# Transposes of a tail's normalized tiles enter TensorE's order 1600 planned nanoseconds later

## The chip, the cores and the metric

The kernel runs on one core of a Trainium2 chip. The metric is the device time of one execution in microseconds (us). One core has five engines with an instruction queue each: TensorE (PE in the profile; its weight loads are listed as PEld), VectorE (DVE), ScalarE (ACT), GpSimd (POOL) and SyncE (SP), which issues most DMA transfers. Every queue is worked off in the order in which the program wrote it; an instruction whose inputs are not there yet holds up all that stands behind it in its queue.

## The reference

The program is one block with adaptive layer norm: an attention followed by a mixer. S = 2048 rows, D = 512 columns, H = 32 heads of 16, F = 1792, all in float32.

```
mod = silu(c) @ w_mod                       # six rows: sa, ca, ga, sb, cb, gb
h = layernorm(x) * (1 + ca) + sa
x = x + ga * attention(h, wqkv, wo)         # softmax over 2048 keys, 32 heads
h = layernorm(x) * (1 + cb) + sb
# mixer B(h):
g  = gelu(layernorm(h) @ w1)                # then four column groups shifted by +1, -1, +2, -2 rows
x1 = h + shifted(g) @ w2
x  = x + gb * (x1 + gelu(layernorm(x1) @ w3) @ w4)
```

## The kernel before

**Tiling.** Rows are worked in four chunks of 512 (ci = 0 to 3), each of four tiles of 128 rows. The attention runs chunk by chunk over units of two heads. What follows the attention in a chunk is called its tail, a generator `tail(ci)` with a second part `rest(ci)`. Float32 products are made of three matmuls on a high and a low part (lines 359, 361 and 363), so every activation that TensorE reads as an operand is first split into two parts: a copy on ACT (line 353) and a subtraction on DVE (line 349).

**The steps of a tail.** The attention's output `osb` is transposed (tile `xT`) and split into `A`. Then, for each of the chunk's four tiles, `wo` (12 matmuls of 512 columns), the residual, two layer norms on DVE and POOL (`tst`, `tmv`, `trs`) and last an ACT operation that writes the normalized tile `xn` (line 1367). Two tiles are a group. The group's eight transposes (`xT` from `xn`, line 1247, in the helper `transposed`) and their split give the operand `A` of w1 for this group; w1 has 48 matmuls of 256 columns per group, each bank of 12 followed by a gelu chain on ACT, DVE and POOL (lines 1438 to 1460). With both groups through w1, w2 (12 matmuls of 512 columns per tile) follows, another layer norm, and another set of normalized tiles ("xn4") in groups of two or three tiles. Their transposes give the operand of w3. `rest(ci)` alternates w3 and w4 over pieces of F and writes the output. In `rest(0)` the weights of w3 and w4 are also split for the first time ("fresh", lines 1210 to 1212) and stored; all later uses load the split ones.

**Who transposes.** Each group's transposes are a generator of their own, `norm_T(ts, key, i)`. There are 15 of them: two "xn" groups in every tail, one "xn4" group in tail 0 and two in each of the others. The xn4 groups of tails 1 to 3 also wait until the tail before has issued all of w3. The tiles `xn` have few buffers (three for each kind, two for one), and a tile's wo is not started while they are taken; `norm_T` gives its buffers free after its transposes are split.

**What sets the order.** No order is left to a compiler. The program plans its own time with a class `Sched`: `T["P"]` is TensorE's planned time, advanced by a cost for each matmul (`nsq`: 0.4405 ns per column and 6) and by 110 ns for a transpose; `T["A"]`, `T["D"]`, `T["G"]` stand for ACT, DVE and POOL. Work for TensorE comes from a list of generators. `one()` walks the list from its head and advances the first generator that can run by one matmul. A generator that yields a function is held until the function says true; one that yields a number has used that much planned time. `spawn` puts `norm_T` at the head of the list, so it goes ahead of everything else once it is free to run. Behind it stand the tails in order, then the `rest` parts. Work for the other engines is a chain of operations with costs, which are written into their engines' queues as planned time passes; `mark` sets a flag (such as ("xn", t): tile t is normalized) when the chain's planned time is reached. All this happens while the program is written. On the chip there is only the resulting order in each queue, and semaphores.

While the attention runs, tail 0 is fed into TensorE's order in portions: `fill(due)` is called behind some blocks of attention work, with a budget of planned time (in the last stretch 1000 ns a block, spent once 1300 have come together). When the attention is over, its PSUM banks are given back, a new PSUM pool is opened, the tails 1 to 3 are put on the list, and `step()` moves planned time on in steps of 100 ns; if no generator can run in a step, planned time passes and nothing is written.

Of the kernel before, what the change touches and what calls it, by code (L numbers as in the profile page):

```python
# [72 lines left out]
W0G = 1  # L73
WSPL = 1
ZPRIO = 2
NPRIO = 1
HOLD = 0
NLOW = 1
# [243 lines left out]
def cD(n=CH):  # L322
    return n / 0.96 + 69
# [7 lines left out]
def kernel(ctx, tc, A_x, A_wqkv, A_wo, B_w1, B_w2, B_w3, B_w4, c, w_mod, out):  # L331
# [89 lines left out]
    sch = Sched()  # L421
# [806 lines left out]
    def transposed(src, ks, nt, A):  # L1228

        n = nt * P  # L1230
        ks = list(ks)
        if n <= 2 * P:
            ks = [ks[i:i + 2] for i in range(0, len(ks), 2)]
        else:
            ks = [[k] for k in ks]
        left = [len(ks)]

        def one():
            left[0] -= 1
        for kk in ks:  # L1240
            yield sch.room
            b = dbank("xT")
            m = len(kk)
            b3 = b[:, :m * n].rearrange("p (k n) -> p k n", k=m)
            for j, k in enumerate(kk):
                for i in range(nt):
                    te.transpose(b3[:, j, i * P:(i + 1) * P], src(k, i), ident)  # L1247
                    yield 110
            k = slice(kk[0], kk[0] + m)
            sch.chain(*split_ops(A[:, k, 0, :n], A[:, k, 1, :n], b3, 1.0, m * n), (None, 0, one), bank=b)  # L1250
        yield lambda: left[0] == 0

    def spawn(gen, key):

        def run():
            yield from gen
            done.add(key)
        sch.add(run(), 0)
# [24 lines left out]
    def tail(ci):  # L1283
# [25 lines left out]
        def tA(nm, i, n):  # L1309

            t = big["A4" if nm == "A4" and not (end and i) or early else "A"]
            o = (2 * P * i if t is big["A4"] or nm == "A" else 0) * 2 * KT
            return t[:, o:o + 2 * KT * n].rearrange("p (k i n) -> p k i n", k=KT, i=2)
# [61 lines left out]
        def normed(key, t, rs):  # L1375
            tag = xtag(key, t)
            xlive[tag] = xlive.get(tag, 0) + 1
            x = xn[key, t] = (tp if tag == "x4" else fa).tile([P, D], F32, name="xn", tag=tag, bufs=XN[tag])
            y = xbt[t]
            return ln_apply(x, y, rs), mark((key, t))  # L1380

        def xtag(key, t):
            if key == "xn":
                return "xn" if early else "xf"
            return "x4" if ci and t in sub[0] else "xn"
# [4 lines left out]
        def norm_T(ts, key, i):  # L1390

            yield lambda: all((key, t) in done for t in ts) and (key == "xn" or not ci or ("w3", ci - 1) in done)
            An[key, i] = A = tA("A4" if key == "xn4" else "A", i, len(ts) * P)
            yield from transposed(lambda k, j: xn[key, ts[j]][:, k * P:(k + 1) * P], range(KT), len(ts), A)
            xlive[xtag(key, ts[0])] -= len(ts)

        for i, t in enumerate(new):
            yield lambda: ci != 1 or i < HOLD or ("xn4", 2) in done
            yield lambda: sch.room() and xn_room("xn", t) and t in x1t and sch.now() >= arr.get(("x1", t), 0.0) and (ci < 2 or ("z", t - 2 * TPC) in done)
            yield from wo_mm(i, range(KT))  # L1400
            b = banks.pop(i)
            x1 = x1t[t]
            xb = xbt[t] = pool_of(ci).tile([P, D], F32, name="xb", tag="xb", bufs=XBF if pool_of(ci) is fa else XBT)

            def x1_add(x1=x1, b=b):
                dve.tensor_tensor(x1, x1, b, op=OP.add)
                sch.free(b)

            r, m, ops = ln_ops(x1, True)
            r2, ops2 = ln_ops(xb)  # L1410

            def center(xb=xb, x1=x1, m=m, ops=ops):
                ops[0][2]()
                sch.late = sch.put("G", 464, sch.T["D"] - cD() + XX, ops[1][2]) + XX
                dve.scalar_tensor_tensor(xb, x1, m[:, 0:1], cbrow, op0=OP.subtract, op1=OP.mult)

            def scale(xb=xb, r=r):
                dve.scalar_tensor_tensor(xb, xb, r[:, 0:1], sbrow, op0=OP.mult, op1=OP.add)

            go = partial(sch.chain, ("D", cD(), x1_add), ("D", 2 * cD() + 150, center), ("D", cD(), scale), *ops2,  # L1420
                         *normed("xn", t, r2), bank=b)
            go()
            if i % 2:
                spawn(norm_T(grp[i // 2], "xn", i // 2), ("T", ci, i // 2))
# [77 lines left out]
        for si, ts in enumerate(sub):  # L1502
            yield lambda: all(("g", ci, i, n) in done for i in range(1 + (t0 + 1 in ts)) for n in range(4))
            for t in ts:
                yield lambda: sch.room() and xn_room("xn4", t)
                b = dbank("w2")
                yield from rows_mm(b, lambda k, p: g[:, k, p, 130 + (t - t0) * P - SH[k]:][:, :P], w, range(KT), KT)
                xb, x1 = xbt[t], x1t[t]

                def xb_add(xb=xb, b=b):  # L1510
                    dve.tensor_tensor(xb, xb, b, op=OP.add)
                    sch.free(b)

                r, ops = ln_ops(xb)
                z = (("D", cD(), lambda xb=xb: dve.scalar_tensor_tensor(xb, xb, 2.0, gbrow, op0=OP.mult, op1=OP.mult)),
                     ("G", cG(), lambda xb=xb, x1=x1: pool.tensor_tensor(x1, x1, xb, op=OP.add)), mark(("z", t)))
                sch.chain(("D", cD(), xb_add), *ops, *normed("xn4", t, r),
                          (None, 0, lambda z=z: sch.chain(*z, prio=ZPRIO)), bank=b, prio=NPRIO)
            spawn(norm_T(ts, "xn4", si), ("T4", ci, si))
# [211 lines left out]
```

## Time and profile before

| | |
|---|---|
| median of 3 runs | 2020.98 us (2018.84 to 2023.25) |
| profiled execution | 2021.44 us |
| its span, first to last instruction | 2019.7 us |
| mean granted TensorE clock | 0.992 |
| TensorE busy | 1934.4 us (96%) |
| DVE, POOL, ACT busy | 1656.3, 1571.9, 1510.2 us |
| instructions | 41655 |

All rows of the prediction come from the profiled execution. In the timeline a row has the start in us from the span's beginning, the duration, the engine, the line of the kernel, the operation, what it writes and from what, and a count where equal neighbours are merged; brackets hold the idle time of the engine just ahead and what ended it. Matmuls are pipelined, so the cost of one in a row of many is the distance from start to start, which is shorter than its duration. The tails 1 to 3 begin at about 1540 us, behind the attention.

### The profile page before, as it was taken

How to read it: one execution, taken by the hardware profiler on the slowest of the kernel's cores; microseconds unless marked ns; L12 is line 12 of the kernel's file. 1: busy time of each engine (PE TensorE's matmuls, PEld its weight loads, DVE VectorE, ACT ScalarE, POOL GpSimd, SP SyncE). 2: the span in 40 equal slices, each digit the busy share in tenths (PEclk: the TensorE clock that was granted, in tenths of full speed). 3: DMA queues.
4: the chain of work that ended last, by engine and by line, in shares of the span. 5: the costliest groups of instructions: out<-in, count | busy, mean ns of one | idle time of the engine just before them, and what ended most of it. 6: DMA issues, size and time to landing. Idle time of an engine off the chain costs nothing.

```text
span 2019.7 us, 41655 instructions
## 1 busy us (share of the span) xinstructions
PE 1934.4 (96%) x14456; PEld 1162.1 (58%) x14456; DVE 1656.3 (82%) x2979; ACT 1510.2 (75%) x3085; POOL 1571.9 (78%) x1488
## 2 busy tenths in 40 slices
PE   7999999999999999999999999999998999999999
PEld 5755545454444444444444444444455878898998
DVE  6398888879999999999999999999975886556443
ACT  6438987768999999999999999999985544344443
POOL 6349988879999999999999999999996554435222
PEclk9989999999999999999999999999999999999999
DMA  8777675445343434444443435354414676553541
GB/s 295 233 204 192 151 187 155 135 130 124 86 92 87 91 88 83 96 82 97 81 98 75 104 72 107 72 136 126 99 46 158 230 261 265 226 200 116 201 153 68
DMA packets 185508, 278.01 MB, mean 138 GB/s; under 512 B 117104, under 2 KB 127856, under 8 KB 169008
## 3 DMA queue, kind: packets, MB, share of 16 engines
q1 hardware_dynamic: 181792, 267.20, 49.1%
q10 hardware_dynamic: 2304, 4.20, 0.6%
q0 software_dynamic: 1200, 3.93, 0.5%
q8 instruction: 115, 1.88, 0.4%
q14 instruction: 97, 0.79, 0.1%
HBM read 211.81 MB, written 62.91 MB: 136 GB/s over the span
## 4 chain that ended last, share of the span: by engine, by line
PE 61%; DVE 16%; ACT 9%; issue 6%; POOL 4%; DMA 3%; SPq 0%; ACTq 0%; POOLq 0%; DVEq 0%
PE mb L996 13%; DVE mx L992 12%; PE pv L1086 9%; PE sc L1012 8%; ACT pt L1008 7%; PE w L363 5%; PE w L359 5%; PE w L361 5%; PE pv L1083 4%; PE ot L1113 3%; POOL pt L1061 2%; PE xT L1247 1%; POOL trs L1356 1%; PE v L359 1%; DMA wr<-Ws 1%
## 5 line engine op out<-in xcount | busy, mean ns | idle before, releaser
L1061 POOL TENSOR_SCALAR pt<-pt 128x1024 f16<-128x1024 uint16 x953 | 1248.3, 1367 | 79.9 <-ACT pt L1008 76.7
L992 DVE TENSOR_REDUCE mx<-mb 128x1 f32<-128x512 f32 x2048 | 1250.0, 681 | 72.7 <-PE mb L996 63.5
L1008 ACT ACTIVATE pt<-sc 128x512 int32<-128x512 f32 x2048 | 1060.9, 614 | 123.5 <-PE mb L996 97.1
L996 PE MATMUL mb<-kst,qtl 62*128 62x512 f32 x2048 | 781.1, 461 | 20.5 <-ACT pt L1008 10.0
L1012 PE MATMUL sc<-qtl,kst 64*128 64x512 f32 x2048 | 739.3, 449 | 4.6 <-DVE mx L992 1.8
L996 PEld LDWEIGHTS mb<-kst,qtl 62*128 62x128 f32 x2048 | 358.9, 193 | 233.7 <-ACT pt L1008 160.4
L1012 PEld LDWEIGHTS sc<-qtl,kst 64*128 64x128 f32 x2048 | 336.6, 185 | 185.4 <-DVE mx L992 118.7
L1086 PE MATMUL pv<-pt,vst 128*32 128x512 f16 x4096 | 384.8, 397 | 20.6 <-ACT ac L1103 20.6
L1460 POOL TENSOR_TENSOR g<-sq,g 128x256 fp32r<-128x256 f32 (+1 forms) x124 | 96.8, 785 | 188.9 <-ACT g L1459 176.6
L1083 PE MATMUL pv<-pt,vst 128*32 128x512 f16 (+1 forms) x2048 | 220.8, 389 | 2.5 <-POOL pt L1061 2.4
L1086 PEld LDWEIGHTS <-vst 128*32 128x32 bf16 x4096 | 91.8, 93 | 227.2 <-issue 208.8
L361 PE MATMUL w<-A,wr 128*128 128x256 f32 (+1 forms) x520 | 153.4, 295 | 0.3 <-DVE A L349 0.3
L359 PE MATMUL w<-A,wr 128*128 128x256 f32 (+1 forms) x520 | 153.2, 295 | 0.3 <-ACT A L353 0.3
L363 PE MATMUL w<-A,wr 128*128 128x256 f32 (+1 forms) x520 | 153.1, 294 | 0.0
L1456 ACT ACTIVATE sq<-w 128x256 f32<-128x256 f32 (+1 forms) x130 | 52.1, 401 | 127.0 <-PE w L363 117.5
L363 PE MATMUL w<-wr,g 128*128 128x512 f32 x270 | 106.5, 394 | 3.1 <-POOL g L1460 3.1
L359 PE MATMUL w<-wr,g 128*128 128x512 f32 x270 | 106.9, 396 | 1.8 <-DMA wr<-Ws 1.8
L361 PE MATMUL w<-wr,g 128*128 128x512 f32 x270 | 106.1, 393 | 0.0
L1438 DVE SCALAR_TENSOR_TENSOR sq<-sq,w 128x256 f32<-128x256 f32 (+1 forms) x130 | 58.1, 449 | 56.5 <-ACT sq L1458 56.3
L359 PEld LDWEIGHTS w<-A,wr 128*128 128x128 f32 x520 | 98.7, 190 | 1.7 <-ACT A L353 0.5
L361 PEld LDWEIGHTS w<-A,wr 128*128 128x128 f32 x520 | 98.7, 190 | 1.6 <-DVE A L349 0.5
L363 PEld LDWEIGHTS w<-A,wr 128*128 128x128 f32 x520 | 98.6, 190 | 0.5 <-issue 0.5
(156 smaller groups left out, 2131.6 us busy)
## 6 DMA issues: line engine op xcount, KB each, us to landing
wr<-Ws SPq DMA_DIRECT2D x66, 1024.0 KB, 5.2
vst<-Vs SPq DMA_DIRECT2D x64, 768.0 KB, 5.7
kst<-Ks SPq DMA_DIRECT2D x126, 384.0 KB, 6.1
Ws<-wr SPq DMA_DIRECT2D x14, 1024.0 KB, 5.0
qtl<-Qs SPq DMA_DIRECT2D x128, 96.0 KB, 4.3
Vs<-vt SPq DMA_DIRECT2D x32, 384.0 KB, 4.2
Ks<-qk SPq DMA_DIRECT2D x16, 512.0 KB, 3.8
Qs<-qk SPq DMA_DIRECT2D x16, 512.0 KB, 3.0
```

The source lines that it names most:

```text
L359: te.matmul(o, lh, rh, start=first, stop=False)
L361: te.matmul(o, lh, rl, start=False, stop=False)
L363: te.matmul(o, ll, rh, start=False, stop=last)
L992: end = sch.crit("D", 605, e + PX, lambda: dve.reduce_max(mxs[u][:, j, g, c:c + 1], b, axis=AX.X))
L996: return ready, lambda: te.matmul(b, lhs, kst[u % 3][r, c * CH:(c + 1) * CH], start=True, stop=True), after
L1008: ea = sch.crit("A", 480, e + PX, lambda: act.activation(pt[s][:, j], b, AF.Exp))
L1012: return ready, lambda: te.matmul(b, kst[u % 3][r, kt * P:(kt + 1) * P], qst[u][r], start=True, stop=True), after
L1061: e_low[s] = XP["G"] + sch.crit("G", 1345, ready, lambda: pool.tensor_scalar(o, i, 0.5, 1.0, op0=OP.mult, op1=OP.mult))
L1083: te.matmul(acc[r:r + n, :], v[:, kt + i, c:c + n].bitcast(F16), pt[s + i].bitcast(F16)[:, j, 0::2], start=False, stop=kt == NKT - 2, skip ...
L1086: te.matmul(acc[r:r + 32, :], v[:, kt, r:r + 32], pt[s].bitcast(F16)[:, j, 1::2], start=kt == 0, stop=False, skip_group_check=True)
L1113: te.matmul(b[:, t * n:(t + 1) * n], ac[:, t * P:(t + 1) * P], smat.rearrange("p j d -> p (j d)"), start=True, stop=True)
L1460: ("G", cG(n), lambda: pool.tensor_tensor(lo, sq, hi, op=OP.subtract)), (None, 0, end), bank=b)
```

## The change

A constant `TW = 1600.0` is added, and one line in `norm_T`. Once all tiles of the group are marked as normalized, the generator is held until TensorE's planned time has advanced by another 1600 ns; only then does it take its buffer and emit transposes. `sch.wait(t)` returns the function that compares planned time with the time of the call plus t. Nothing else is edited, and every group in every tail is treated alike.

```diff
 ZPRIO = 2
+TW = 1600.0
 NPRIO = 1
...
         def norm_T(ts, key, i):

             yield lambda: all((key, t) in done for t in ts) and (key == "xn" or not ci or ("w3", ci - 1) in done)
+            yield sch.wait(TW)
             An[key, i] = A = tA("A4" if key == "xn4" else "A", i, len(ts) * P)
             yield from transposed(lambda k, j: xn[key, ts[j]][:, k * P:(k + 1) * P], range(KT), len(ts), A)
             xlive[xtag(key, ts[0])] -= len(ts)
```

## The prediction

> **What bounds the kernel now.** I read the page first, then the list of who waited for whom, then TensorE's timeline around each wait, since the change only moves TensorE work.
>
> ```profile
> span 2019.7 us, 41655 instructions
> PE 1934.4 (96%) x14456; PEld 1162.1 (58%) x14456; DVE 1656.3 (82%) x2979; ACT 1510.2 (75%) x3085; POOL 1571.9 (78%) x1488
> ```
>
> TensorE bounds the kernel: it is busy 96% of the span, so a change of order can only win what is left of idle time, or open more. The list of waits says who causes the idle time (total us, times, longest us).
>
> ```profile
> PE xT L1247 <- ACT xn L1367: 14.1, 9, 2.9
> ...
> PE w L363 <- POOL g L1460: 3.1, 2, 2.2
> ...
> PE w L359 <- DMA wr<-Ws: 1.8, 3, 0.9
> ```
>
> In the tails the transposes (xT, line 1247) that wait for the last normalized tile (xn, line 1367) hold most of it: 14.1 us in 9 waits. These are the instructions that the change moves. The timeline shows the nine waits, one of another kind ahead of them, and one group that waits for nothing (start, duration, what; in brackets the idle time before it).
>
> ```profile
> 1539.93 1.09 PE L1247 MATMUL xT<-ident,xn 128*128 128x128 f32 x8 [2.25 <-DVE sq L1438]
> ...
> 1558.70 0.33 PE L1247 MATMUL xT<-ident,xn 128*128 128x128 f32 x1 [0.56 <-ACT xn L1367]
> 1560.60 0.33 PE L1247 MATMUL xT<-ident,xn 128*128 128x128 f32 x1 [1.57 <-ACT xn L1367]
> 1563.87 2.40 PE L1247 MATMUL xT<-ident,xn 128*128 128x128 f32 x10 [2.94 <-ACT xn L1367]
> ...
> 1582.53 0.98 PE L1247 MATMUL xT<-ident,xn 128*128 128x128 f32 x7 [1.54 <-ACT xn L1367]
> ...
> 1605.38 0.98 PE L1247 MATMUL xT<-ident,xn 128*128 128x128 f32 x7 [2.52 <-ACT xn L1367]
> ...
> 1659.21 0.98 PE L1247 MATMUL xT<-ident,xn 128*128 128x128 f32 x7 [1.40 <-ACT xn L1367]
> ...
> 1707.28 0.98 PE L1247 MATMUL xT<-ident,xn 128*128 128x128 f32 x7 [2.04 <-ACT xn L1367]
> ...
> 1790.40 1.91 PE L1247 MATMUL xT<-ident,xn 128*128 128x128 f32 x16
> ...
> 1818.00 0.98 PE L1247 MATMUL xT<-ident,xn 128*128 128x128 f32 x7 [0.59 <-ACT xn L1367]
> ...
> 1832.26 0.98 PE L1247 MATMUL xT<-ident,xn 128*128 128x128 f32 x7 [0.98 <-ACT xn L1367]
> ```
>
> Read with the code, 1558.70 to 1563.87 is tail 0's three-tile second group; 1582.53 and 1605.38 are tail 1's first two groups, 1659.21 and 1707.28 tail 2's, 1818.00 and 1832.26 tail 3's. Each waits because the planner counts the chain from a matmul to its normalized tile shorter than it runs.
>
> **The change part by part.** It adds no instruction and no wait on the chip. The planner's wait only lets other generators emit for 1600 planned ns first. Where none can, TensorE's order stays as it is and the cost is nothing, since planned idle time emits nothing. Where one can, that many matmuls go ahead of the transposes. How many follows from the steps between starts.
>
> ```profile
> 1580.36 0.33 PE L361 MATMUL w<-A,wr 128*128 128x384 f32 x1
> 1580.53 0.34 PE L363 MATMUL w<-A,wr 128*128 128x384 f32 x1
> ...
> 1608.20 0.28 PE L359 MATMUL w<-A,wr 128*128 128x256 f32 x1
> 1608.32 0.28 PE L361 MATMUL w<-A,wr 128*128 128x256 f32 x1
> ```
>
> A step is 0.17 us at 384 columns and 0.12 us at 256, so 1.6 us is 10 or 14 matmuls. With a step of 0.23 us at 512 columns (below) it is 7.
>
> *Tail 0's groups before 1545.* The group at 1539.93 waits 2.25 us for DVE, where the PSUM pool is closed; w1's second half needs these transposes and nothing else is open, so I take 0. The first group stands in the attention; it is the slower rival below.
>
> *Tail 0's three-tile group (1558.70).* When its last tile is normalized, wo of tail 1 opens in the same planned moment and now goes first.
>
> ```profile
> 1557.76 0.39 PE L363 MATMUL w<-wr,g 128*128 128x512 f32 x1
> ...
> 1565.92 0.78 PE L359 MATMUL wo<-wr,A 128*128 128x512 f32 x1
> 1566.49 0.63 PE L361 MATMUL wo<-wr,A 128*128 128x512 f32 x1
> 1566.92 0.63 PE L363 MATMUL wo<-wr,A 128*128 128x512 f32 x1
> ...
> 1569.89 0.40 PE L359 MATMUL wo<-wr,A 128*128 128x512 f32 x1
> 1570.12 0.40 PE L361 MATMUL wo<-wr,A 128*128 128x512 f32 x1
> ...
> 1606.12 0.36 PE L361 MATMUL w<-A,wr 128*128 128x256 f32 x1
> ...
> 1562.50:1563.00 0.50, 0.00 (x0) 1.00 0.00 0
> 1563.00:1563.50 0.50, 0.00 (x0) 0.52 0.84 45
> ```
>
> Before, w2 ends at 1558.15 and TensorE does almost nothing until 1563.87. After, 7 wo matmuls run there: 7 x 0.23 = 1.6 us won. The transposes still end with the third tile. The last two rows are half-microsecond windows (PE busy, granted clock): the clock falls to half at about 1563.0, 4.9 us after w2's end. Nine wo matmuls from 1565.92 to 1569.89 then take 3.97 us where 9 x 0.23 = 2.1 would do, and ten transposes 2.05 us (1563.87 to 1565.92) where the rate of 1605.38 (seven in the 0.74 us to the next matmul at 1606.12) makes 1.1: 1.9 + 1.0 = 2.9 us. After the change the stretch shrinks to 1563.87 - 1559.8 = 4.1 us, under the 4.9 after which the clock fell, so I count 2.9 us won; the ends are 0 and 2.9. The Trainium skill, "TensorE: Matmul & The Clock Gate", section "Why this matters for your kernels", speaks against this term: by it a gap over about 3 us already sends the clock to half. By that rule the 2.9 us are not won and the sum below is 2015.6; the trace does not decide, since 2.52 us at 1605.38 is its longest other gap here.
>
> *Tail 1, first group (1582.53).* w3 of tail 0 is cut in two by these transposes; 10 of its matmuls, 1.7 us, go first and cover the wait of 1.54.
>
> *Tail 1, second group (1605.38).* Behind it stand 5 matmuls of w1 from 1606.12, 6 of w4 and 12 more of w1, then w1 of this very group, which needs the copies of the transposes.
>
> ```profile
> 1606.80 0.40 PE L361 MATMUL w<-wr,g 128*128 128x512 f32 x1
> ...
> 1608.00 0.69 DVE L349 TENSOR_TENSOR A<-xT,A 128x512 fp32r<-128x512 f32 x1 [0.30 <-ACT A L353]
> ...
> 1608.94 0.68 DVE L349 TENSOR_TENSOR A<-xT,A 128x512 fp32r<-128x512 f32 x1
> ```
>
> 5 x 0.12 + 5 x 0.23 = 1.8 us go ahead, so 1.8 of 2.52 is won. But the copies end at 1609.62, 3.5 us after the transposes leave at 1606.12, and only 0.23 + 12 x 0.12 = 1.7 us of cover is left; the first half of A is there at 1608.69 and carries six matmuls (0.7 us), so about 1.0 is lost again: 0.8 us. The ends are 0 and 1.8.
>
> *Tail 2, first group (1659.21).* w3 is cut here too: 10 matmuls go first, 1.40 us won.
>
> *Tail 2, second (1707.28), and both of tail 3 (1818.00, 1832.26).* 14 matmuls of w1, 7 of w4 and 14 of w1 go first: 1.6, 0.59 and 0.98 us, 3.2 together. Of tail 2's w1, 17 matmuls (2.0 us) stay behind the transposes.
>
> *The groups that wait for w3 (as at 1790.40).* There was no wait to win. w4 now stands directly behind w3 and needs its activations.
>
> ```profile
> 1790.11 0.74 POOL L1460 TENSOR_TENSOR g<-sq,g 128x256 fp32r<-128x256 f32 x1 [0.69 <-ACT g L1459]
> ```
>
> The last one its first tile needs is done at 1790.85, 0.3 us after w3's end (about 1790.56), and three w4 matmuls run without it: 0.
>
> The moved step issues transposes, an ACT copy and a DVE subtraction per bank, no POOL operation and no DMA. On ACT and DVE its copies pass behind some activations. SP's weight loads hang on w1's end and move with it.
>
> **The sum.** The first stretch (1558 to 1660) gives 1.6 + 2.9 + 1.5 + 0.8 + 1.4 = 8.2 us, the rest 3.2. The first stretch will not keep it all.
>
> ```profile
> 1558.00:1660.00 102.00, 88.31 (x472) 77.64 (x471) 85.78 (x166) 51.41 (x104) 61.62 (x81) 0.97 0.64 227
> 1660.00:1860.00 200.00, 195.54 (x1202) 175.00 (x1201) 126.58 (x263) 86.20 (x207) 86.00 (x131) 1.00 0.57 210
> ```
>
> Columns are length, then busy PE, weight loads, DVE, ACT, POOL. DVE works 85.8 of 102 us in the first stretch, almost as long as TensorE, since it also splits fresh weights there; at 102 - 8.2 us it would be 91% busy, and TensorE already waits there for POOL (2.2 us) and a weight load (0.9). What TensorE wins, those waits can take back. Ends: none and all of the 8.2; with nothing that decides I take half, 4.1. From 1660 to 1860 TensorE works 195.5 of 200 us and DVE 126.6, and the waits to be won are most of the 4.5 us left; with DVE at 63% nothing stands ready to take them back, so those 3.2 stay. Against the profiled execution's 2021.44 us, which stands 0.5 us above the median of the runs, the time is 2021.44 - 4.1 - 3.2 = 2014.1 us, said as 2014.
>
> **The rivals.** *Nothing is taken back:* 2021.44 - 11.4 = 2010 us; with no loss at tail 1's second group 2009. For it: most of the work moved ahead stood ready. Against: DVE's 91%.
>
> *The gain is handed back:* the first stretch stays as long as it was, because it is the fresh weights and DVE that time it, and only the 3.2 stay: 2018.2; if the splits open in the later tails too, 2021. For it: the POOL wait of 2.2 us in that stretch. It also covers the case that the planner finds nothing to put ahead. Against: the groups at 1582.53, 1659.21 and 1818.00 cut a run of matmuls in two.
>
> *Slower: tail 0's first group misses its slot in the attention.* There TensorE takes tail work only in budgeted portions.
>
> ```profile
> 1512.04 1.08 PE L1113 MATMUL ot<-smat,ac 128*128 128x34 f32 x8
> ...
> 1517.35 1.09 PE L1247 MATMUL xT<-ident,xn 128*128 128x128 f32 x8
> ...
> 1521.48 0.50 PE L359 MATMUL wo<-wr,A 128*128 128x512 f32 x1
> ...
> 1527.46 0.50 PE L359 MATMUL wo<-wr,A 128*128 128x512 f32 x1
> ...
> 1538.30 0.81 ACT L1367 ACTIVATE xn<-xb,trs 128x512 f32<-128x512 f32 x1 [0.19 <-POOL trs L1361]
> ```
>
> The portion at 1517.35 holds only the transposes. If 1600 ns carry them past it, they come 4.1 us later, at 1521.48, and wo of tile 3, which needs one of their three buffers, moves to 1527.46, 6.0 us later. Then the tile at 1538.30 and all of tail 0 behind the attention come up to 6.0 us late; the attention ends earlier by the portion not spent, 9 x 0.23 = 2.1, so the price is 3.9 to 6.0 us. Alone it makes 2014 into 2018 to 2020. It decides when the first stretch keeps nothing as well: 2021.44 + 6.0 - 3.2 = 2024 us. The portion before, at 1512.04, took other work and not this group, so I take it that the group became ready within those 5.3 us, and 1.6 of 5.3 is a third.
>
> **How the numbers follow.** The forecast has 0.50, with a range of its own from 2010 to 2017. No loss has 0.12, handed back 0.22, slower 0.16: half of the third in which the slot is missed, since both must meet. If the clock falls all the same, the forecast moves by half of 2.9, to 2015.6, inside its range; I give that 0.4 of the 0.50. Measurement tells a change of 0.2%, 4 us, from none: faster is 0.50 + 0.12 = 0.62, the same 0.22, slower 0.16. The range reaches from 2009 to 2024.
>
> **What would show it.** Right: the waits of xT for xn fall from 14.1 us to under 6; wo stands ahead of the transposes at 1558; the granted clock stays at 1.00 near 1565; w3, w1 and w4 matmuls stand ahead of the groups of tails 1 to 3. Wrong: new waits of w (lines 359 to 363) for A, g or weight loads of over 4 us between 1558 and 1660; the first group later than 1520; DVE without gaps from 1600 to 1660.

## The result and the profile after

The changed kernel takes 2028.27 us (median; 2026.28 to 2033.08), the kernel before, on the same chip beside it, 2020.98 (2018.11 to 2024.23). The ratio is 1.0041, with a 95% interval from 1.003 to 1.0053: about 8 us slower. The prediction said 2014 and faster. The profiled execution took 2026.73 us.

The page of the changed kernel begins so:

```profile
span 2023.8 us, 41655 instructions
PE 1939.6 (96%) x14456; PEld 1168.5 (58%) x14456; DVE 1656.9 (82%) x2979; ACT 1510.1 (75%) x3086; POOL 1569.9 (78%) x1487
```

No instruction was added to TensorE, but it is busy 5.2 us longer (1939.6 for 1934.4): the same matmuls ran more often at half clock. The list of who waited for whom (total us, times, longest us; lines are one or two higher than before) shows which waits were exchanged:

```profile
PE xT L1248 <- ACT xn L1368: 9.4, 6, 3.4
...
PE w L360 <- DMA wr<-Ws: 6.2, 3, 5.2
PE xT L1248 <- DVE sq L1440: 3.4, 1, 3.4
PE w L364 <- POOL g L1462: 3.1, 3, 1.8
```

The waits of transposes for normalized tiles fell by 4.7 us, from 14.1 to 9.4. The wait for loads of split weights rose by 4.4 (1.8 to 6.2), most of it one wait of 5.2 us, and the one at the closing of the PSUM pool by 1.1. TensorE's timeline of the changed kernel has them in place:

```profile
1515.90 1.09 PE L1248 MATMUL xT<-ident,xn 128*128 128x128 f32 x8
...
1536.07 1.09 PE L1248 MATMUL xT<-ident,xn 128*128 128x128 f32 x8 [3.38 <-DVE sq L1440]
...
1558.12 0.40 PE L360 MATMUL wo<-wr,A 128*128 128x512 f32 x1
...
1562.47 2.40 PE L1248 MATMUL xT<-ident,xn 128*128 128x128 f32 x10 [2.94 <-ACT xn L1368]
...
1584.45 0.50 PE L364 MATMUL w<-wr,g 128*128 128x512 f32 x1 [1.75 <-POOL g L1462]
1585.88 0.50 PE L364 MATMUL w<-wr,g 128*128 128x512 f32 x1 [0.46 <-POOL g L1462]
...
1606.52 0.98 PE L1248 MATMUL xT<-ident,xn 128*128 128x128 f32 x7 [1.92 <-ACT xn L1368]
1610.93 0.38 PE L360 MATMUL w<-A,wr 128*128 128x256 f32 x1 [0.29 <-ACT A L354]
1611.66 0.38 PE L362 MATMUL w<-A,wr 128*128 128x256 f32 x1 [0.34 <-DVE A L350]
...
1624.06 0.79 PE L360 MATMUL w<-wr,g 128*128 128x512 f32 x1 [5.15 <-DMA wr<-Ws]
...
1666.76 1.50 PE L1248 MATMUL xT<-ident,xn 128*128 128x128 f32 x7 [3.37 <-ACT xn L1368]
...
1714.00 0.99 PE L1248 MATMUL xT<-ident,xn 128*128 128x128 f32 x7 [0.41 <-ACT xn L1368]
...
1825.84 1.03 PE L1248 MATMUL xT<-ident,xn 128*128 128x128 f32 x8
...
1840.21 1.04 PE L1248 MATMUL xT<-ident,xn 128*128 128x128 f32 x8
```

From the top: tail 0's first group; the group at the closing of the pool (its wait was 2.25); wo ahead of the three-tile group; that group's last tile; tail 1's w4 waiting for POOL behind the first group, which itself no longer waits; tail 1's second group (2.52 before) and the waits for its copies; the second piece of tail 1's w2 (0.94 before); tail 2's first group (1.40 before); its second (2.04 before); tail 3's two, without a wait.

Where did the time go by stages? The table takes the end of the last transposes of osb ahead of w1 of tail 0 as zero point (1489.09 in the trace of before, 1483.48 in that of after), since the attention ahead of it ran 5.6 us quicker in the second profiled execution: no edit stands behind that, and in the other twelve executions profiled below the point lies between 1484.6 and 1488.9. (3.0 of the 5.6 us arise between 290 and 330 us, where the clock fell for 6.83 us in the execution of before and not in that of after.)

| stage | before, us | after, us | difference |
|---|---|---|---|
| to the end of tail 0's w1 | 58.88 | 63.22 | +4.34 |
| to the first w3 of tail 0 | 28.05 | 26.17 | -1.88 |
| to the start of tail 1's w2 | 39.32 | 44.50 | +5.18 |
| tail 1's w2 | 12.46 | 19.16 | +6.70 |
| to the first run of 96 matmuls of 256 columns (1739.65 before) | 111.85 | 108.86 | -2.99 |
| to the end | 276.32 | 274.76 | -1.56 |

The sum is +9.79, and less the 5.61 of the attention +4.2, the difference of the spans. In the third stage stand 10 w3 and 8 w4 matmuls more than before (10 x 0.17 + 8 x 0.23 = 3.5 us), which the fifth does not have to do: without them the third lost about 1.6 us, and the fifth lost 0.6. Three stages carry the loss: tail 0's w1, tail 1's way to w2, and w2 itself.

Windows of the changed kernel (length, busy PE with its count, granted clock, DMA share, GB/s) show the half clock:

```profile
1537.00:1544.00 7.00, 6.55 (x30) 0.53 0.27 111
1561.50:1568.00 6.50, 5.53 (x18) 0.50 0.98 353
...
1623.00:1629.50 6.50, 5.44 (x13) 0.50 0.27 112
1667.50:1670.00 2.50, 2.50 (x9) 0.50 0.65 262
```

Before, there was one such stretch behind the attention (1563.02 to 1569.85); now there are four. The first of the four is not the change's alone: of eleven executions whose order is that of before up to this place, eight fall there too, and the profiled one of before is among the three that do not.

### The profile page after: what moved, and what is told of

The parts are those of the page before. It is cut to its first block, busy times and chain, and to the rows that moved or that the text cites. A ratio compares the mean times of both kernels' runs of the same rounds, so it can differ in the third digit from the quotient of the medians.

```text
span 2023.8 us, 41655 instructions
## 1 busy us (share of the span) xinstructions
PE 1939.6 (96%) x14456; PEld 1168.5 (58%) x14456; DVE 1656.9 (82%) x2979; ACT 1510.1 (75%) x3086; POOL 1569.9 (78%) x1487
## 4 chain that ended last, share of the span: by engine, by line
PE 59%; DVE 17%; ACT 10%; issue 6%; POOL 3%; DMA 3%; SPq 1%; ACTq 0%; POOLq 0%; DVEq 0%
PE mb L997 13%; DVE mx L993 12%; PE pv L1087 9%; PE sc L1013 8%; ACT pt L1009 7%; PE w L362 5%; PE w L360 5%; PE w L364 5%; PE pv L1084 4%; PE ot L1114 3%; POOL pt L1062 2%; DMA wr<-Ws 1%; PE xT L1248 1%; POOL trs L1357 1%; SPq L136 1%
## 5 line engine op out<-in xcount | busy, mean ns | idle before, releaser
L360 PE MATMUL w<-wr,g 128*128 128x512 f32 x270 | 108.5, 402 | 6.2 <-DMA wr<-Ws 6.2
L364 PE MATMUL w<-wr,g 128*128 128x512 f32 x270 | 107.9, 400 | 3.1 <-POOL g L1462 3.1
L362 PE MATMUL w<-wr,g 128*128 128x512 f32 x270 | 107.6, 399 | 0.0
```

The lines of the kernel that those rows point to most:

```text
L360: te.matmul(o, lh, rh, start=first, stop=False)
L362: te.matmul(o, lh, rl, start=False, stop=False)
L364: te.matmul(o, ll, rh, start=False, stop=last)
```

## The experiments

Ratios are to runs of the kernel before on the same chip. What each kernel changes is shown with it; the computation is whole in all of them. The ratio is an estimate over all runs of the comparison and not the quotient of the two medians; where the text turns a ratio into us, it takes it times 2020. The mean granted clock is that of all timed runs of the kernel, not of the profiled one.

| kernel | median, us | ratio (95%) | mean clock |
|---|---|---|---|
| before (medians of the four comparisons) | 2019.62 to 2020.98 | | 0.9910 |
| changed | 2028.27 | 1.0041 (1.003 to 1.0053) | 0.9879 |
| wait in tail 0's w1 groups only | 2020.28 | 1.0015 (1.0005 to 1.0025) | 0.9906 |
| wait in tail 0's three-tile group only | 2026.28 | 1.0036 (1.0024 to 1.0048) | 0.9885 |
| wait in tail 1's w1 groups only | 2030.21 | 1.0051 (1.0038 to 1.0063) | 0.9882 |
| wait in tails 2 and 3 only | 2017.07 | 0.9988 (0.9979 to 0.9997) | 0.9910 |
| changed, two stores later | 2023.80 | 1.0019 (1.0009 to 1.0028) | 0.9902 |
| before, two stores behind the load | 2020.09 | 1.0000 (0.9991 to 1.0009) | 0.9914 |
| before, two stores ahead of the load | 2023.06 | 1.0018 (1.0004 to 1.0032) | 0.9912 |
| before, clock kept up in tail 0 | 2022.02 | 1.0005 (0.999 to 1.0019) | 0.9908 |
| tails 2 and 3, clock kept up | 2022.70 | 1.0016 (1.0006 to 1.0027) | 0.9908 |
| tail 1's w1 groups, stores later | 2027.42 | 1.0030 (1.0015 to 1.0045) | 0.9891 |
| changed but tail 0's w1 groups, stores later | 2021.26 | 1.0007 (0.9998 to 1.0017) | 0.9907 |
| tail 0's three-tile group, tails 2 and 3, stores later | 2019.05 | 0.9998 (0.999 to 1.0007) | 0.9901 |

### One tail at a time

Four kernels make the wait conditional; the condition is all that differs. For tail 0's w1 groups:

```diff
-            yield sch.wait(TW)
+            yield from [sch.wait(1600.0)] if not ci and key == "xn" else []
```

*Tail 0's w1 groups.*

> The wait stands only in tail 0's two first groups (those behind wo). Theory, from the trace of the changed kernel: the first group misses its portion in the attention, w1's first half bunches up at the attention's end, the wait for the new PSUM pool grows from 2.25 to about 3.4 us and the granted clock falls to half for about 7 us behind it: 3 to 4 us slower than before (ratio about 1.0017), with the weight load of tail 1's w2 waited for as before (0.9 us). Rival 1, the whole loss of 7 us sits in this missed portion: 6 to 8 us slower. Rival 2, the missed portion is harmless because TensorE is full there: within 1 us of before.

Measured: ratio 1.0015, about 3 us slower (1 to 5), as expected. The eleven runs reach from 2019.1 to 2027.1 us, and with so few the value hangs on the estimate: the median stands only 0.2 us above that of before, the mean 2.1. The timeline of this kernel has the changed kernel's wait where the pool is closed:

```profile
1517.01 1.09 PE L1247 MATMUL xT<-ident,xn 128*128 128x128 f32 x8
...
1537.15 1.12 PE L1247 MATMUL xT<-ident,xn 128*128 128x128 f32 x4 [3.38 <-DVE sq L1438]
```

From the zero point of the stages the first group comes 32.4 us later here and in the changed kernel (1517.01 - 1484.61; 1515.90 - 1483.48), before 28.3 (1517.35 - 1489.09): it missed its portion and took the next, 4.1 us on. How much of the +4.34 of the first stage is due to it? Eleven executions profiled in this study have the order of before up to that stage's end; they take 58.86 to 61.43 us, 60.3 on average. The three with the group moved take 61.73, 62.81 and 63.22, on average 62.6. So the group costs about 2.3 us; the rest of the +4.34 is that the profiled execution of before was among the quickest there. Part of the 2.3 is again the clock, which fell at the pool's closing in all three and in eight of the eleven. Among executions with a fall of 3.41 us there the stage takes 61.7 with the group moved and 60.3 without, among those with one of 6.83 us 63.0 and 61.2: 1.4 to 1.8 us for the same fall.

*Tail 1's w1 groups* (condition `ci == 1 and key == "xn"`).

> The wait stands only in tail 1's two first groups. Theory: planned time moves on, the load of w2's second weight piece comes to stand behind two 1 MB stores in SP's queue, TensorE waits about 5 us for it instead of 0.9, and the clock falls behind that wait; against it stand 1.5 to 2 us won at the transposes: 4 to 6 us slower than before. Rival 1, the loss is the missed portion in the attention: no loss here, 1 to 2 us faster. Rival 2, the splits behind the transposes lose their cover: 1 to 2 us slower, with waits of w for A and not for the weight load.

Measured: 10 us slower (8 to 13), more than the whole change and more than the 4 to 6 expected. Its timeline repeats the wait for the second piece of w2:

```profile
1627.11 0.80 PE L359 MATMUL w<-wr,g 128*128 128x512 f32 x1 [4.96 <-DMA wr<-Ws]
```

*Tails 2 and 3* (condition `ci >= 2`).

> The wait stands in all groups of tails 2 and 3 and nowhere else. Theory: the waits of the second group of tail 2 and of both groups of tail 3 go (2.0, 0.6 and 1.0 us before) and nothing comes in their place: 2.5 to 4 us faster than before. Rival 2, splits lose their cover in every tail: 1 to 3 us slower.

Measured: ratio 0.9988, 2.4 us faster (0.6 to 4.2), at the low edge of what was expected. Its groups at 1657, 1816 and 1830 wait for nothing; ahead of the one at 1657, the wait of w4 for POOL's g stays as it was (2.23 before):

```profile
1650.43 0.50 PE L363 MATMUL w<-wr,g 128*128 128x512 f32 x1 [2.17 <-POOL g L1460]
...
1657.02 1.04 PE L1247 MATMUL xT<-ident,xn 128*128 128x128 f32 x8
...
1815.92 1.03 PE L1247 MATMUL xT<-ident,xn 128*128 128x128 f32 x8
...
1830.29 1.04 PE L1247 MATMUL xT<-ident,xn 128*128 128x128 f32 x8
```

This is the one part that pays, and the only kernel here that is faster than the kernel before by more than the noise.

*Tail 0's three-tile group* (condition `not ci and key == "xn4"`).

> The wait stands only in tail 0's three-tile group. Theory: seven matmuls of wo run ahead of the transposes, 1.6 us won, and the clock falls to half all the same, so the prediction's further 2.9 us do not come: 1 to 2 us faster than before, unless a later order on SP or DVE changes. The prediction's step: the clock stays at 1.00 and 4 to 4.5 us are won. Rival: the lead is handed back at tail 1's weight loads, no difference.

Measured: 7 us slower (5 to 10), against an expected gain of 1 to 2. Seven wo matmuls did go ahead. But tail 1's second group then waits 2.89 us for its normalized tiles, the w2 piece 3.44 and tail 2's first group 4.46, and the clock falls five times behind the attention. Here one store of split weights stands ahead of the w2 load in SP's queue; in the changed kernel and in the one with tail 1 alone there are two; in the kernels of tail 0's w1 groups and of tails 2 and 3 there is none, as before. The cost goes roughly by that number (7, 8 and 10 us with stores ahead; 3 lost and 2.4 won without), which made the place of the stores the suspect.

### The stores ahead of the load

The rows of SP's queue, before:

```profile
1612.66 0.34 SPq L135 DMA_DIRECT2D wr<-Ws  x1
1614.88 0.34 SPq L135 DMA_DIRECT2D Ws<-wr  x1
```

```profile
1617.82 0.50 PE L359 MATMUL w<-wr,g 128*128 128x512 f32 x1 [0.94 <-DMA wr<-Ws]
```

and in the changed kernel:

```profile
1613.06 2.09 SPq L136 DMA_DIRECT2D Ws<-wr  x2
1615.24 2.64 SPq L136 DMA_DIRECT2D wr<-Ws  x2
```

Before, the load is written first and lands by the time TensorE's wait ends at 1617.82: 5.2 us after its issue. After, two stores of 1 MB from the splitting of fresh weights stand ahead; the second waits for DVE to finish splitting, and the load is issued at 1615.24 and lands at 1624.06, 8.8 us later. The planner's wait had moved tail 1's w1, and with it the point at which the load of the next piece is written, to behind those stores.

*The changed kernel with the two stores written 4000 planned ns later.*

```diff
-                sch.dma(dma.dma_start, Ws[i], w.bitcast(F32))
+                st = lambda: sch.dma(dma.dma_start, Ws[i], w.bitcast(F32))
+                sch.after(sch.T["P"] + 4000.0, st) if i in (6, 15) else st()
```

> The changed kernel with one further edit: the two stores of split weights that in the changed kernel stand in SP's queue ahead of the load of w2's second piece in tail 1 are written 4000 planned ns later, behind that load. Nothing else moves. Theory (the stores stretch that load from 5.1 to 8.6 us): TensorE's wait for the w2 piece in tail 1 falls from 5.15 to about 1 us, w2(1) takes 12.5 to 13 us instead of 19.2, the clock does not fall inside it, and the time is 4 to 7 us below the changed kernel's 2028.3, about 2022. Rival (the w2 wait only takes the place of an idle time that comes anyway, for POOL's g or for normalized tiles): the wait goes, another of 4 us or more stands behind it before 1700 us, and the time stays within 2 us of 2028.3.

Measured: ratio 1.0019 where the changed kernel has 1.0041. The difference, 0.0022 or 4.4 us (0.0022 +- 0.0015 from the two intervals), is in the expected 4 to 7. SP's queue has the load first, and TensorE's wait falls from 5.15 to 2.34 us. The load is issued no earlier than behind the stores (1615.21 for 1615.24), so what their place costs is the time to its landing:

```profile
1615.21 0.33 SPq L135 DMA_DIRECT2D wr<-Ws  x1
1615.63 0.38 SPq L135 DMA_DIRECT2D Ws<-wr  x1
```

```profile
1621.77 0.80 PE L359 MATMUL w<-wr,g 128*128 128x512 f32 x1 [2.34 <-DMA wr<-Ws]
```

The details missed: the wait was to be about 1 us, and w2 took 15.3 us, not 12.5 to 13, because the load lands 6.6 us after issue and not 5.2, and because one clock fall (1621.58 to 1625.00) still lies in it. Why 6.6? Ten of the kernels of this document have no store ahead of this load. In seven of them SP issues the next transfer within 1 us behind it, and it lands 6.5 to 6.8 us after its issue; in three the next one follows 2.1 us later or more, as in the kernel before, and it lands after 5.0 to 5.3. So a transfer close behind goes with about 1.4 us, and the two stores ahead with 2.2 more. The kernel of tails 2 and 3 is one of the seven:

```profile
1609.01 0.34 SPq L135 DMA_DIRECT2D wr<-Ws  x1
1609.97 0.34 SPq L135 DMA_DIRECT2D Ws<-wr  x1
```

*Is it shared bandwidth or the place in the queue?* Two kernels add two stores of 1 MB that nothing reads to the kernel before, the one directly behind the load and the other directly ahead of it:

```diff
                 else:
+                    for x in extra.pop(0) if i == 12 and extra else ():
+                        dma.dma_start(x, sbrow[:, None, :].to_broadcast([P, 4, D]))
                     sch.dma(dma.dma_start, w.bitcast(F32), Ws[i])
```

(In the kernel with the stores behind, the two new lines stand below the last one.)

> The kernel before, with two extra stores of 1 MB each to scratch memory that nothing reads, written into SP's queue directly behind the load of w2's second piece in tail 1. The load keeps its place and its issue time; only what moves beside it grows. Theory A (shared bandwidth stretches the load): its landing goes from 5.1 us to 8 us or more, TensorE's wait for it from 0.94 to 3 to 5 us, and the time is 4 to 7 us above before when the clock falls in that wait, 2 to 4 when not. Theory B (it is the place in the queue that counts: a load behind stores is issued later): wait and time are as before, within 1 us.

> The kernel before, with the same two extra 1 MB stores as in the run with them behind, now directly ahead of the load of w2's second piece in SP's queue. TensorE's order is that of before. Theory (a load waits for the transfers written ahead of it; 1 MB takes about 3 us): the load lands 8 to 9 us after its issue instead of 5.2 to 6.6, TensorE's wait for it is 4 to 5 us instead of 0.94, and the time is 3 to 5 us above before. Rival (the long landing comes from how the changed kernel's work is arranged, not from the stores): wait under 2.5 us, time within 1 us of before.

Measured: behind, no change of the time (ratio 1.0000, 0.9991 to 1.0009). Ahead, 1.0018 (1.0004 to 1.0032), 3 us at the median (0.8 to 6.5 by the interval). With the stores behind:

```profile
1608.28 0.34 SPq L135 DMA_DIRECT2D wr<-Ws  x1
1608.67 1.35 SPq L1168 DMA_DIRECT2D Xs<-sbrow  x2
```

```profile
1614.81 0.50 PE L359 MATMUL w<-wr,g 128*128 128x512 f32 x1 [2.31 <-DMA wr<-Ws]
```

and with the stores ahead:

```profile
1606.85 1.91 SPq L1167 DMA_DIRECT2D Xs<-sbrow  x2
1610.33 0.34 SPq L135 DMA_DIRECT2D wr<-Ws  x1
```

```profile
1619.97 0.79 PE L359 MATMUL w<-wr,g 128*128 128x512 f32 x1 [5.41 <-DMA wr<-Ws]
```

Behind, the load lands 6.5 us after its issue (1614.81 - 1608.28), as in the kernel of tails 2 and 3, where one store follows it closely and the wait is 2.38. Ahead, it lands after 9.6 us and the wait is 5.41, both a little over what was expected. Neither theory of the first run is right as it stands: the wait grew from 0.94 to 2.31, not to 3 to 5 as shared bandwidth had it, and it did not stay as the place in the queue had it. Transfers close behind the load make it about 1.4 us longer, which did not show in the median; the same stores ahead make it 3.1 us longer again, and that did. Whether they must stand in the same queue for this, or only be under way earlier, no run here shows, since none writes the stores into another queue. The Trainium skill, "DMA: Bandwidth & Descriptors", section "Two DMAs through the same engine are not ordered", says that within one queue of a DMA engine descriptors start in order; the order of landings in these two runs agrees.

*Tail 1's w1 groups with the stores late.*

> The wait of 1600 planned ns for tail 1's two w1 groups alone (10 us slower when tried by itself), with the two stores written behind the load of w2's second piece. Theory (the place of the stores makes most of the loss): wait for the w2 piece 2 to 2.5 us instead of 4.96, time 4 to 5 us above before instead of 10. Rival (the other waits that it opens, for POOL's g and tail 2's normalized tiles, make most of it): 8 to 10 us above before.

Measured: 1.0030 instead of 1.0051. The wait is 2.42 us, as expected, and 4 us of the 10 went (0 to 8, from the two intervals). The loss that stays, 6 us (3 to 9), is between the two expectations: by these values the stores are less than half of what tail 1 costs.

*The changed kernel without tail 0's w1 groups and with the stores late.*

> The changed kernel without the wait in tail 0's two w1 groups, and with the two stores behind the load of w2's second piece. Theory (the first group costs about 3 us, the stores about 4.5 us, and they add up): within 1.5 us of before. Rival (what is not lost there is lost in the waits behind): 3 to 5 us above before, as with the stores late and the first group moved.

Measured: 1.0007 (0.9998 to 1.0017), 1.2 us at the median: as the theory of two causes has it. Beside the kernel with only the stores late (1.0019) the first group is worth 0.0012 +- 0.0013, 2.4 us, as by the stages above but not clear of noise by itself. Taken at these values, 4.4 of the 8 us belong to the stores and 2.4 to the first group; about 1.4 are left. If the parts added up, tail 1 and the three-tile group would still cost about 4 in it, since tails 2 and 3 win 2.4 by themselves.

*Only the parts that seemed to win.*

> The wait of 1600 planned ns for tail 0's three-tile groups and for tails 2 and 3, the two stores behind the load; tail 0's and tail 1's w1 groups as before. Theory (only the parts that win: wo ahead of the transposes at 1558, 2 us, and the later tails, 2.4): 3 to 4.5 us faster than before. Rival (what is won at 1558 is lost again to tail 1's normalized tiles and the w2 piece): 1 us slower to 2.4 us faster.

Measured: 0.9998 (0.999 to 1.0007), inside the rival's range; the w2 piece has no part in it (its wait is 0.77 us). The second stage, with wo ahead of the transposes, is 3.1 us shorter (25.0 for 28.05), and the third, in which no order was meant to change, 2.4 longer (41.7 for 39.3). TensorE gets to tail 1's groups earlier, and their tiles are not ready earlier by as much:

```profile
1578.32 0.98 PE L1248 MATMUL xT<-ident,xn 128*128 128x128 f32 x7 [1.89 <-ACT xn L1368]
...
1600.88 1.75 PE L1248 MATMUL xT<-ident,xn 128*128 128x128 f32 x7 [2.86 <-ACT xn L1368]
```

Before, these two waits were 1.54 and 2.52. They explain 0.7 of the 2.4; behind the second the clock is at half from 1600.79 to 1604.20, which it was not before, and 3.41 us of work at half clock cost at most 1.7.

### The clock

*The kernel before, with spare matmuls between the transposes of tail 0's three-tile group* (4, 12 and 24 of 128 columns, from a tile at hand into PSUM columns that nothing reads):

```diff
+                    for _ in range(warm[i] if warm and k == 0 else 0):
+                        te.matmul(b[:, 384:512] if nt == 3 else b[:, 128:256], g1["t"][:, 0, 0, 130:258],
+                                  g1["t"][:, 0, 0, 130:258], start=True, stop=True)
```

> The kernel before, with 4, 12 and 24 spare matmuls of 128 columns between the transposes of tail 0's three-tile group, whose results nothing uses. Nothing else is added or moved. Theory (transposes and idle time alike let the clock fall, in whole windows of 3.41 us, two of which are lost there; matmuls keep it up): the granted clock stays at 1.00 from 1555 to 1575 us, w2 of tail 0 to wo of tail 1 run at full rate, and the time falls by about 3 us (2 to 3.4). Rival (what follows waits for normalized tiles or weights anyway): the clock stays up, wo ends as late as before, time within 1 us of before.

Measured: ratio 1.0005 (0.999 to 1.0019). The clock stayed up where it was meant to, and fell elsewhere:

```profile
1555.00:1575.00 20.00, 19.41 (x117) 1.00 0.49 171
1600.50:1607.00 6.50, 5.45 (x20) 0.50 0.64 220
1709.50:1712.50 3.00, 3.00 (x16) 0.50 0.02 5
```

In its own stage the expected 3 us came: to the first w3 of tail 0 it takes 24.98 us for 28.05. The time is the rival's all the same, though not for the rival's reason, that wo would end as late as before. The mean clock over its runs is that of before (0.9908 and 0.9910). The timeline shows where it goes: with wo done sooner, tail 1's second group waits 3.25 us for its tiles (2.52 before), and the clock falls there. The twelve runs reach from 2015.5 to 2028.17 us, wider than those of before beside them (2016.28 to 2025.14); so what the spare matmuls win seems to be kept in some runs and lost in others.

*The wait in tails 2 and 3, with spare matmuls in tail 0 and also in tail 1.*

> The wait of 1600 planned ns for the groups of tails 2 and 3 alone (2.4 us faster when tried by itself), with the spare matmuls of the run above in tail 0's three-tile group, and 14 more in tail 1's two w1 groups. Theory (the parts are independent): 2.4 + 3 + up to 1 us faster than before, 2014 to 2016. Rival (what is won early is handed back to weight loads in tail 1, whose wait was already 2.38 us with the wait in tails 2 and 3 alone): 2016 to 2019.

Measured: 1.0016, a miss by both. In tail 1 the spare matmuls waited 3.30 us for their own operand, a tile that ACT was just rewriting, so this run says nothing of the theory.

## Why the prediction was wrong

*The step that failed* is a half sentence: "SP's weight loads hang on w1's end and move with it". They move with it, but past two stores of 1 MB in SP's queue. The load of w2's second piece landed 8.8 us after its issue instead of 5.2, and TensorE waited 5.15 us for it instead of 0.94. Writing the stores behind it, where it lands after 6.6, gives back 4.4 of the 8 us (1.4 to 7.4). With this step fell the bounds of the discount, "none and all of the 8.2": they let the waits behind take back at most what was won, while w2 of tail 1 alone became 6.70 us longer and the way to it 1.6. The range's end of 2024 stood on these bounds. The step before, that the transposes issue no DMA, was right and not enough: the order between the moved step and what other generators write into the same queue changed.

*Tail 0's first group*, the slower rival, came true: it took the next portion, 4.1 us later. The price of 3.9 to 6.0 was too high; 2.4 (by two kernels, +- 2.7) to 3.0 (by itself, 1 to 5) was measured. The wait at the pool's closing grew only from 2.25 to 3.38. Its share of a third was read off the spacing of portions, but the order is fixed when the program is written, so it was never a matter of chance on the chip.

*Tail 0's three-tile group.* The seven wo matmuls went ahead, and the second stage is 1.88 us shorter: 1.6 was right. (Over all executions without spare matmuls it takes 25.4 us with this part of the change and 27.2 without.) The 2.9 for the clock was wrong. I had taken 4.9 us from the last matmul to the fall for a threshold; after the change the stretch is 4.1 and the clock fell all the same, at 1561.27, and 1561.50 to 1568.00 is at 0.50. In the trace of before, w2 ends at 1558.15 and the clock falls at 1563.02; by the grid of the last section the unit of 3.413 us up to 1563.02 is the first one in which TensorE did next to nothing (one transpose), and the 4.9 us are only what was left of the unit before, and one whole unit. The Trainium skill's rule quoted against this term came out right here.

*Tail 1, first group.* The 1.54 of wait went as said, and w4 behind it then waited 1.75 + 0.46 for POOL's g, which the term did not have: 0.7 lost instead of 1.5 won.

*Tail 1, second group.* 1.92 of the 2.52 stayed (0.7 was forecast), and 0.29 + 0.34 for the copies came new: nothing won, instead of 0.8.

*Tail 2, first group.* 1.40 was to be won; the wait is now 3.37 us, while a wait of w4 for POOL's g of 2.23 ahead of it is gone. Together 3.63 before and 3.58 (with 0.21 at the first tile) after: what goes is not the wait, only its name. It belongs to the chain from wo to the normalized tile: from wo's end to the end of this wait it takes 18.2 us before (1641.01 to 1659.21) and 18.3 after (1648.51 to 1666.76), though TensorE does other work in between. By itself the term was right: in the kernel of tails 2 and 3, where tail 1 is as before, the transposes start 18.2 us after wo's end (1638.80 to 1657.02) without a wait, since ten w3 matmuls fill the time, and the 2.17 for POOL's g stays. With the edit in tail 1 alone, this wait is already 3.35 us: the 10 w3 and 8 w4 matmuls counted below the table of stages have then run before wo and are missing behind it.

```profile
1652.70 0.50 PE L363 MATMUL w<-wr,g 128*128 128x512 f32 x1 [2.23 <-POOL g L1460]
```

*Tail 2, second, and tail 3.* Right. 2.04 became 0.41 (1.6 won), 0.59 and 0.98 became 0, and the last stage is 1.56 us shorter. Alone, tails 2 and 3 make the kernel 2.4 us faster (0.6 to 4.2); the terms for their groups, with the 1.40 of tail 2's first, come to 4.6. The groups that wait for w3 cost nothing, as said.

*The discount of half* had the right idea and a wrong culprit and size. I named DVE, 91% busy:

```profile
1558.00:1660.00 102.00, 88.57 (x457) 77.08 (x456) 79.47 (x152) 45.64 (x94) 54.33 (x71) 0.93 0.60 217
```

DVE is busy 79.5 of 102 us in the first stretch, less than the 85.8 before. It was the weight load, POOL's g and the chain of the layer norm that took back all of the 8.2, and more.

*The signs named ahead.* The waits of xT fell to 9.4, not under 6; wo stands ahead at 1558; w3, w1 and w4 stand ahead of the later groups; the clock near 1565 did not stay up; new waits of w over 4 us between 1558 and 1660 came. DVE without gaps did not: from 1600 to 1660 it is busy 42.2 of 60 us. The sign "first group later than 1520" was badly put: it came at 1515.90 only because the attention ended 5.6 us earlier, and is 4.1 later by its own stage.

*What the clock adds.* Over all timed runs, a lower mean clock by 0.001 goes with 1.23 us more within one kernel. The changed kernel's mean clock is 0.0031 below that of before: 3.8 of the 8 us go with it. Brought to the same clock, the single edits are +1.5 (tail 0's w1 groups), +5.9 (tail 1), +3.2 (tail 0's three-tile group) and -2.6 (tails 2 and 3) against the runs of before beside them, together 8.0, where the whole change has 4.2 (8 - 3.8; its clock of before is taken from the other comparisons). The falls follow for the most part from the new waits, so this is no cause beside them; it says in what form half of the loss appears. What stays open is how tail 1's 6 us with the stores late divide among POOL's g, the load and the falls: in the full change, beside the other tails' groups, a part of it does not appear, so the parts do not add up.

## What to carry to other kernels

A step moved in a hand-planned order moves everything that its generator writes later, in every queue: list, for each DMA queue, what it is moved past, above all large stores ahead of a load that an engine will wait for. A wait that ends a long chain on other engines isn't won by putting other work ahead of it unless that work would otherwise have run after the chain's end; look for the next consumer of the same chain and ask if its input will be earlier too. Where the tail is bound only by TensorE, as in tails 2 and 3 here, the same edit does pay, so an edit made everywhere is worth splitting by place.

## What the runs showed of the hardware

The clock falls and rises on a grid. In the profiled execution of after it falls at 1537.37, 1561.27, 1622.71 and 1667.08 us and rises at 1544.20, 1568.09, 1629.53 and 1670.49, read from half-microsecond windows that hold the change, such as these:

```profile
1537.00:1537.50 0.50, 0.19 (x3) 0.87 1.00 426
1561.00:1561.50 0.50, 0.00 (x0) 0.77 0.00 0
1622.50:1623.00 0.50, 0.00 (x0) 0.71 0.97 410
1667.00:1667.50 0.50, 0.50 (x5) 0.58 0.05 16
```

(A mean of 0.87 in half a microsecond that starts at 1 and ends at 0.5 puts the fall 0.37 us into it.) All distances are multiples of 3.413 us: 7, 18 and 13 between the falls, and each of these cold spells is one or two units. Near the start of the same execution there is one of three (10.24 us from 96.95). The grid begins elsewhere in each execution. The Trainium skill, "TensorE: Matmul & The Clock Gate", section "Part 1: The HAM clock gate (the "warmup" mystery)", gives a free-running window of 3413 ns; the trace agrees.

So time since the last matmul does not decide by itself. Behind 1500 us the fourteen traces of this document have 31 waits of TensorE of 2.86 to 5.41 us, and every one has a fall in it or within one unit behind it; of the 39 from 2.03 to 2.62 us 15 have one and 24 have none. What separates them is how much work lies in one unit. An estimate from the rows of all fourteen traces between 1500 and 1950 us, with a matmul or transpose counted from its start to the next start, at most to its end: of 48 units at full clock with up to 1.54 us of work (45% of a unit) 47 end in a fall, of 1700 with more only 2 do, both at the pool's closing. So a wait around 2 us costs a fall or none by where it lies on the grid, which for the most part also explains why the same order at the pool's closing fell in one execution and not in another.

In the kernel before, the window from 1537 to 1544 is at full clock; in the run of before with two stores behind the load, same order, it is not:

```profile
1537.50:1541.50 4.00, 3.83 (x19) 0.57 0.50 207
```

In the unit from 1557.86 to 1561.27 TensorE worked at wo until 1558.36 and then made only two of the transposes, 1.1 us of work in all, and the clock fell at its end. What decides whether it stays low for one unit or two is open.
